# Split products for the last 64 rows of two expert passes, weight buffers dealt anew

## The chip, the cores and the metric

The kernel runs on one core of a Trainium2 chip. The metric is the device time of one execution in microseconds (us). Five engines of the core work side by side, each on its own queue of instructions: TensorE (PE; its weight loads are listed as PEld), VectorE (DVE), ScalarE (ACT), GpSimd (POOL) and SyncE (SP), which only issues DMA transfers. The matrix sums are collected in PSUM, eight banks of 128 x 512 fp32.

## What is computed

The reference takes pooled queries through an attention, sends each of the 1152 resulting rows of 512 values to one of eight experts, and ends in a feed-forward layer. The part around the change is the experts:

```
logits = xc @ w_gate                      # xc: rows with x @ w_skip > 0
e_idx = argmax(logits)
for e in range(8):
    mask = e_idx == e
    h = maximum(xc[mask] @ w1[e], 0.0)    # w1[e]: 512 x 1024
    y[mask] = gate_w[mask] * (h @ w2[e])  # w2[e]: 1024 x 512
out[do_compute] = xc + y
```

All of it is fp32. A matmul with fp32 operands is exact enough; the kernel also uses split products: an operand is the sum of a high and a low half of type fp32r, and three matmuls (high by high, high by low, low by high; the tuple PASS) stand for one.

## The kernel before

The attention ends at about 232 us, the routing and the experts run from there to about 358 us, and the feed-forward layer from there to the end. Rows are sorted into groups of at most 32 rows for each expert (the small groups), and for the experts 0 and 2 into wide passes: 320 rows for expert 0 (two tiles of 128 and a tail of 64), 192 rows for expert 2 (one tile of 128 and a tail of 64). The order of the work on each engine is that of the program text (the schedule is written by hand), and an engine waits for whatever its next instruction needs.

Weights lie in 32 loads of 1 MB, w0 to w31: load n is quarter n % 4 of expert n // 4, the first two quarters W1, the others W2. `place(n)` gives each a buffer, and a load waits until the last reader of the buffer's former content is done. `load_w(first, stop)` issues such loads on SyncE, in that order, so that one that waits holds up those behind it. `whi(e, i)` makes the high half of a quarter on ScalarE, `wlo(e, i)` the low half on VectorE (line 1393), both into spare buffers of the same pool that later loads take over: whi(0, i) in 7 + i, wlo(0, i) in 3 + i, whi(2, i) in 5 + i, wlo(2, i) in 7 + i.

`routing` counts and ranks the rows. It calls `second`, which fetches the rows of the first wide pass on GpSimd, makes wlo(0, 0) and wlo(0, 1), transposes the small rows into xsT[0] and makes the hidden products of the small groups 0 and 1 (`up`, line 645). In `moe`, `turn` transposes such hidden products on TensorE (line 786) and copies them out (line 790); `down`, called by `small2`, multiplies them by W2 (line 807) and adds the two halves on VectorE (line 816); `prep` transposes one tile of a wide pass and makes its high half on ScalarE (line 713) and low half on VectorE (line 714), in the PSUM tag "am", which has two buffers.

`wide` is a loop over nine steps. Step fc makes the hidden products of chunk fc of 128 hidden columns (line 728), runs a hook if one is given for it, and adds the output products of chunk fc - 1 (lines 745 and 750). The hidden products of expert 0 are split products, those of expert 2 plain fp32 ones. The output products of the 128-row tiles are split (line 745: high and low half of the activation are made at lines 733 and 734). Those of the tail are plain fp32 from the raw W2, in two halves of 256 columns that go into the two halves of a PSUM bank's partitions:

```
for half in range(2):
    nc.tensor.matmul(
        acc[J][MID * half : MID * half + MID, :256], g[2],
        wts[e, 2 + fc // 4][:, fc % 4, 256 * half : 256 * half + 256],
```

When a pass ends, its sums are copied out and scattered to the rows of ytok in device memory by GpSimd (line 691), one scatter after another. When the last scatter of expert 2 and that of the small groups 0 to 3 have landed, SyncE loads the first rows of ytok back into yt (line 988), and VectorE adds them to the rows (line 1001), which the feed-forward layer transposes first. Between stand the small groups 4 to 7, which use w16 to w31, and the first loads of the feed-forward weights into a ring (line 1071), whose high halves ScalarE makes and whose low halves VectorE makes (lines 1079 and 1086).

Of the kernel before, what the change touches and what calls it, by code (L numbers as in the profile page):

```python
# [7 lines left out]
F32 = mybir.dt.float32  # L8
F32R = mybir.dt.float32r
AF = mybir.ActivationFunctionType  # L10
ALU = mybir.AluOpType
# [10 lines left out]
P = 128  # L22
# [4 lines left out]
SMALL = 32  # L27
MID = 64
# [10 lines left out]
COL = {r: 2 + i for i, r in enumerate(ROWS)}  # L39
# [441 lines left out]
        nc.tensor.matmul(out, io["ones"], io["blank"], start=True, stop=True)  # L481


def routing(tc, io, lg, rt, tmp, ps, first, second, kept):
    nc = tc.nc
    cst = io["cst"]
    c = lambda n: cst[:, CST[n]]
# [3 lines left out]
    lg = lg[:, :9]  # L491
# [91 lines left out]
    def onehot(cs):  # L583
        n = cs.stop - cs.start
        v = Bm[:, :, cs]
        tt(
            v, c("c128")[:, cs].unsqueeze(1).to_broadcast([P, T, n]),
            hi.unsqueeze(2).to_broadcast([P, T, n]), op=ALU.is_equal,
        )
        tt(v, v, c("tok").unsqueeze(2).to_broadcast([P, T, n]), op=ALU.mult)  # L590
# [9 lines left out]
        column(NEAR, t, ix)  # L600
    nears = tokens(NEAR, ix[:, NEAR])
    keep_warm(nc, io, warm, WARM[5])
    second(idx, ps)
    nc.vector.tensor_copy(cnt[:, :E], count)
    most = sb([P, E + 1], F32, "r_most")
    nc.vector.tensor_copy(most[:, :E], count)
# [3 lines left out]
    nc.vector.tensor_copy(cnt[:, 2 * E :], most[:, E:])  # L610
    stt(cnt[:, E : 2 * E], count, float(-SMALL), thr, op0=ALU.add, op1=ALU.subtract)
    onehot(far)
    ix = ps.tile([P, 512], F32, name="ix", tag="am", bufs=2)
    for t in range(T):
        column(far, t, ix)
# [41 lines left out]
def place(n):  # L657
    if n < 9:
        return 0, n
    if n < 12:  # L660
        return 1, n - 9
    if n < 20:
        return 0, n - 12
    if n < 24:
        return 1, n - 17
    if n < 28:
        return 0, n - 24
    return 1, n - 21


def source(io, e, i):
# [7 lines left out]
def passes(nc, tc, io, r, rows, ytok, wts, ps, wk, nreg, xs, wait=None):  # L679
# [3 lines left out]
    def scatter(src, col, n=P, odd=0):  # L683
        if odd:
            ix = r["odd"][:, col - TAILS.start : col - TAILS.start + 1]
        else:
            ix = r["sidx"][:n, col : col + 1]
        put(src, ix)
# [24 lines left out]
            nc.scalar.copy(xT[:, :, c], tp[:, :, :n])  # L713
            nc.vector.tensor_tensor(lo[:, :, c], tp[:, :, :n], xT[:, :, c].bitcast(F32), op=ALU.subtract)

    def wide(e, xT, w1, w2, outs, hooks):
        J = DEEP[e]
        n = P * J + MID
        two = len(w1) == 2
        acc = [ps.tile([P, 512], F32, name="ly", tag="yl")]  # L720
        acc += [ps.tile([P, 512], F32, name="lt", tag="mt", bufs=2) for _ in range(J)]
        gs = {}

        def hidden(fc):
            a = ps.tile([P, 512], F32, name="la", tag="am", bufs=2)[:, :n]
            prods = [(k, i) for k in range(4) for i in (PASS if two else ((0, 0),))]
            for m, (k, (u, v)) in enumerate(prods):
                nc.tensor.matmul(
                    a, w1[u][k // 2][:, k % 2, P * fc : P * fc + P], xT[v][:, k, :n],
                    start=(m == 0), stop=(m == len(prods) - 1),  # L730
                )
            g = [wk.tile([P, 2 * P], F32R, name=x, tag=x)[:, : P * J] for x in ("wh", "wl")]
            nc.scalar.activation(g[0], a[:, : P * J], AF.Relu)
            nc.vector.scalar_tensor_tensor(
                g[1], a[:, : P * J], 0.0, g[0].bitcast(F32), op0=ALU.max, op1=ALU.subtract
            )
            g.append(wk.tile([P, MID], F32, name="wt", tag="wt"))
            nc.scalar.activation(g[2], a[:, P * J :], AF.Relu)  # L738
            gs[fc] = g

        def outp(fc):
            g = gs.pop(fc)
            for j in range(J):
                for m, (u, v) in enumerate(PASS):
                    nc.tensor.matmul(
                        acc[j], g[u][:, P * j : P * j + P], w2[v][fc // 4][:, fc % 4],
                        start=(fc == 0 and m == 0), stop=(fc == 7 and m == 2),
                    )
            for half in range(2):
                nc.tensor.matmul(  # L750
                    acc[J][MID * half : MID * half + MID, :256], g[2],
                    wts[e, 2 + fc // 4][:, fc % 4, 256 * half : 256 * half + 256],
                    start=(fc == 0), stop=(fc == 7), skip_group_check=True,
                )

        for fc in range(9):
            if fc < 8:
                hidden(fc)
            if fc in hooks:
                hooks[fc]()  # L760
            if fc > 0:
                outp(fc - 1)
        for j in range(J):
            (nc.scalar.copy if j % 2 == 0 else nc.vector.tensor_copy)(outs[j], acc[j])
            scatter(outs[j], COL[e, j])
        for half in range(2):
            (nc.scalar.copy if half else nc.vector.tensor_copy)(
                outs[J][:MID, 256 * half : 256 * half + 256], acc[J][MID * half : MID * half + MID, :256]
            )
        scatter(outs[J][:MID], COL[e, None], MID)  # L770

    def transp(dst, src, alt):
        tp = ps.tile([P, 4, P], F32, name="mt", tag="mt", bufs=2)
# [8 lines left out]
    def turn(M, hs, tag, hT=None):  # L782
        n = M // 16
        tp = ps.tile([P, 4, P], F32, name="ht", tag=tag + "t", bufs=1 if tag == "s" else 2)
        for u in range(n):
            nc.tensor.transpose(tp[:, u], hs[:, P * u : P * u + P], io["ident"])
        if M == SMALL:
            hT = wk.tile([P, n, P], F32, name="hsT", tag="hTs")
        if M == SMALL:
            nc.vector.tensor_copy(hT, tp[:, :n])  # L790
# [100 lines left out]
def moe(tc, io, r, rows, ytok, slot, early, xr, yg, ylast, pick, last, xsT, ps, xm0, hs0, wts, whi, wlo):  # L891
    nc = tc.nc
    with ExitStack() as ctx:
# [42 lines left out]
        def prep0(j):  # L936
            p["prep"](0, j, (xr[:, 1], xr[:, 2], xm0)[j], *xT)

        hT = turn(SMALL, hs0[0], "s")
        prep0(0)  # L940
        small2(0, hT)
        hT = turn(SMALL, hs0[1], "s")
        prep0(1)
        small2(1, hT)
        p["transp"](xsT[1], yg[:, 1], 1)
        gather(yg[:, 1], COL[2, None])
        prep0(2)
        wlo(0, 2)
        wlo(0, 3)
        load_w(12, 14)  # L950
        load_w(16, 20)
        hs = {}

        def next2():
# [5 lines left out]
                p["prep"](2, j, yg[:, j], x2[0])  # L960

        x2 = []
        two = lambda e, i: [[w.w[e, i], w.w[e, i + 1]] for w in (whi, wlo)]
        p["wide"](
            0, xT, two(0, 0), two(0, 2), (xr[:, 1], xr[:, 2], xm0), {2: lambda: r["gates"](r["gate"]), 8: next2}
        )
        load_w(14, 16)
        load_w(20, 24)
        hT = turn(SMALL, hs[2], "s")
        hs[3] = small1(3)  # L970
# [1 line left out]
        for i in (2, 3):  # L972
            wlo(2, i)

        def last3():
            small2(3, turn(SMALL, hs[3], "s"))
            load_w(24, 28)

        def next4():
            hs[4] = small1(4)  # L980

        p["wide"](2, x2, [[wts[2, 0], wts[2, 1]]], two(2, 2), (yg[:, 0], yg[:, 1]), {0: last3, 8: next4})
        load_w(28, 32)
        scatter(ys[0], 0)
        early.open(8)
        nc.sync.dma_start(xr, tiles3(rows, 0))
# [320 lines left out]
def body(tc, io, out):  # L1307
    nc = tc.nc
    with ExitStack() as ctx:
# [59 lines left out]
        with ExitStack() as c2:  # L1369
# [26 lines left out]

            whi.w, wlo.w = {}, {}

            def second(idx, ps):
                fetch(nc, rows, idx, xr[:, 1], COL[0, 0])  # L1400
                fetch(nc, rows, idx, xr[:, 2], COL[0, 1])
                fetch(nc, rows, idx, xm0, COL[0, None])
                wlo(0, 0)
                wlo(0, 1)
                tp = ps.tile([P, 4, P], F32, name="mt", tag="mt", bufs=2)
                for k in range(4):
                    nc.tensor.transpose(tp[:, k], yg[:, 0, P * k : P * k + P], io["ident"])
                nc.scalar.copy(xsT[0], tp)
                for e in range(2):
                    up(nc, ps, hs0[e], SMALL, xsT[0][:, :, SMALL * e : SMALL * e + SMALL], (wts[e, 0], wts[e, 1]), "s")  # L1410

            ps = c2.enter_context(tc.tile_pool(name="m_ps", bufs=1, space=PSUM, reuse_waits="tile"))
            with ExitStack() as c3:
                tmp = c3.enter_context(tc.tile_pool(name="m_rt", bufs=1, reuse_waits="tile"))
                for i in range(4):
                    whi(0, i)
                r = routing(tc, io, lg, rt, tmp, ps, first, second, kept)
# [88 lines left out]
```

## Time and profile before

| what | value |
|---|---|
| time, median of 3 runs | 575.62 us (575.34 to 575.75) |
| the profiled execution | 575.21 us |
| its span, first to last instruction | 573.4 us |
| TensorE busy | 541.2 us, 94% of the span |
| VectorE busy | 389.8 us, 68% |
| ScalarE busy | 372.8 us, 65% |
| DMA | 102.17 MB, mean 178 GB/s |

Busy shares are averages over stages with different limits: in the expert stage TensorE has idle time, in the attention and in the feed-forward layer hardly any. The granted clock of TensorE is given as a share of its full speed of 2.4 GHz; its other level is 1.2 GHz. In a timeline a line of TensorE gives the start, the time to the end, the source line, the tile written and the tiles read, and the form of the array (128\*128, 128\*64, 128\*32). Consecutive matmuls overlap, so the distance from start to start is what one costs, not its own duration. A plain fp32 matmul stands as two records.

### The profile page before, as it was taken

Reading aid. Unit: us, or ns where it says so; the run is one execution under the profiler, and the core shown is the slowest. Engines: PE = TensorE matmul, PEld = TensorE weight load, DVE = VectorE, ACT = ScalarE, POOL = GpSimd, SP = SyncE. Lnnn points to the kernel's source line nnn. Section 1 sums busy time; section 2 is a strip of 40 time slices with the busy share of each in tenths; the row PEclk is TensorE's granted clock in tenths of the full one; section 3 lists DMA queues with packets and bytes.
Section 4 is the critical chain, followed back from the end, with each engine's and each line's share of the span. In section 5 each row is a group of like instructions: output and inputs, shape, how many; then the busy total and the mean of one; then the engine's idle time right before and its main releaser. Section 6 shows DMA issues by size and latency. Waiting matters only on the chain. (4 is left out here: it accounts for less than half of the span.)

```text
span 573.4 us, 11951 instructions
## 1 busy us (share of the span) xinstructions
PE 541.2 (94%) x4788; PEld 405.3 (71%) x4788; DVE 389.8 (68%) x733; ACT 372.8 (65%) x686; POOL 95.7 (17%) x87
## 2 busy tenths in 40 slices
PE   8799999999999999979979969999999999999994
PEld 4566666766676667457746635889899999989882
DVE  3588898888988887863141134799986676666663
ACT  3888888888888885621141222899887667676662
POOL 1223354334533311330001001000000000000000
PEclk9999999999999999999998996999999999999998
DMA  7568868997978771289359594264203100010001
GB/s 259 203 240 280 290 212 285 329 320 250 317 244 302 248 254 58 81 299 390 133 195 404 182 366 150 100 235 135 61 19 102 64 1 1 1 58 0 1 0 60
DMA packets 50113, 102.17 MB, mean 178 GB/s; under 512 B 13995, under 2 KB 15403, under 8 KB 50048
## 3 DMA queue, kind: packets, MB, share of 16 engines
q1 hardware_dynamic: 47760, 95.99, 48.1%
q0 software_dynamic: 1056, 2.97, 1.6%
q10 hardware_dynamic: 1232, 2.36, 1.2%
q8 instruction: 39, 0.64, 0.5%
q14 instruction: 26, 0.21, 0.1%
HBM read 84.70 MB, written 17.04 MB: 177 GB/s over the span
## 5 line engine op out<-in xcount | busy, mean ns | idle before, releaser
L152 DVE TENSOR_SCALAR_CACHE_REDUCE scp<-s 128x1152 f32<-128x1152 f32 x72 | 97.7, 1357 | 34.2 <-PE s L149 20.4
L1187 PE MATMUL ph<-xT,wi 128*128 128x384 f32 x576 | 108.5, 337 | 0.0
L1187 PEld LDWEIGHTS ph<-xT,wi 128*128 128x128 f32 x576 | 102.1, 188 | 4.2
L163 ACT ACTIVATE scp<-scp,mx 128x1152 f32<-128x1152 f32 x72 | 90.5, 1257 | 8.3 <-DVE scp L152 8.1
L149 PE MATMUL s<-ks,qs 64*128 64x288 f32 (+1 forms) x640 | 89.0, 426 | 5.2 <-DVE scp L152 4.9
L1241 PE MATMUL po<-wo,gh 128*128 128x512 f32 x288 | 90.3, 394 | 0.7 <-ACT gh L1226 0.5
L202 ACT COPY eT<-tp 128x1024 f32<-128x1024 f32 x63 | 63.8, 1013 | 27.6 <-PE tp L179 27.0
L220 PE MATMUL ov<-eT,vt 128*64 128x288 f32 x540 | 78.3, 417 | 0.0
L149 PEld LDWEIGHTS s<-ks,qs 64*128 64x128 f32 (+1 forms) x640 | 48.4, 175 | 40.5 <-DVE scp L152 16.6
L1241 PEld LDWEIGHTS po<-wo,gh 128*128 128x128 f32 x288 | 52.9, 188 | 10.2 <-ACT gh L1226 1.4
L1241 PE MATMUL po<-wo,gl 128*128 128x512 f32 x144 | 57.2, 397 | 0.0
L179 PEld LDWEIGHTS tp<-cst,scp 64*128 64x128 f32 x1145 | 47.0, 138 | 13.2 <-issue 3.9
L1211 ACT ACTIVATE u<-u 128x384 f32<-128x384 f32 (+1 forms) x49 | 25.4, 519 | 46.5 <-DVE u L1205 46.0
L1231 DVE TENSOR_TENSOR gl<-s,gh 128x384 fp32r<-128x384 f32 (+1 forms) x49 | 27.0, 550 | 41.7 <-ACT gh L1226 41.5
L351 POOL TENSOR_TENSOR g<-wd 128x512 f32<-128x512 f32 x32 | 34.0, 1062 | 89.0 <-PE s L149 74.8
L179 PE MATMUL tp<-cst,scp 64*128 64x64 f32 x1145 | 48.2, 223 | 0.0
L220 PEld LDWEIGHTS ov<-eT,vt 128*64 128x64 f32 x540 | 33.6, 136 | 19.1
L807 PE MATMUL sy<-w,hsT 128*32 128x256 f32 x256 | 20.3, 472 | 12.4 <-ACT wt L738 4.9
L1241 PEld LDWEIGHTS po<-wo,gl 128*128 128x128 f32 x144 | 27.0, 187 | 6.7 <-DVE gl L1231 1.0
L1205 DVE TENSOR_SCALAR u<-ph 128x384 f32<-128x384 f32 (+1 forms) x49 | 26.7, 546 | 6.4 <-PE ph L1187 6.3
L1213 ACT ACTIVATE r<-s,one 128x384 f32<-128x384 f32 (+1 forms) x49 | 30.0, 612 | 1.6
L1212 ACT ACTIVATE s<-u,one 128x384 f32<-128x384 f32 (+1 forms) x49 | 29.9, 611 | 1.6
(198 smaller groups left out, 752.8 us busy)
## 6 DMA issues: line engine op xcount, KB each, us to landing
w<-w SPq DMA_DIRECT2D x32, 1024.0 KB, 10.3
wd<-wq SPq DMA_DIRECT2D x32, 512.0 KB, 5.1
wdec<-g SPq DMA_DIRECT2D x32, 256.0 KB, 4.3
vt<-vt SPq DMA_DIRECT2D x8, 576.0 KB, 5.9
ks<-kt SPq DMA_DIRECT2D x15, 288.0 KB, 6.9
ring<-wdec SPq DMA_DIRECT2D x16, 256.0 KB, 3.9
wr<-wdec SPq DMA_DIRECT2D x16, 256.0 KB, 2.9
xr<-qt SPq DMA_DIRECT2D x7, 576.0 KB, 5.4
```

What stands on the lines that cost most here:

```text
L149: st["tick"] = nc.tensor.matmul(s[o, half, j, :HQ], w[r], st["k", h, b][r, cs], start=True, stop=True).ins
L152: nc.vector.tensor_scalar(scp.rearrange("p (a c) -> p a c", a=4), s.rearrange("p a j c -> p (a j) c")[:, :, :HQ], -EXP_SCALE, -NEG, op0=AL ...
L163: nc.scalar.activation(scp, scp, AF.Exp, bias=mx, scale=-1.0, accum_out=st["sum", h][:, t : t + 1],)
L179: nc.tensor.matmul(to, e[q, P * i : P * i + P], io["ident"][q, q], start=i < 8 or a != opened, stop=True, is_transpose=True, skip_group_ch ...
L202: nc.scalar.copy(to.rearrange("p k (a c) -> p a k c", a=2), v)
L220: nc.tensor.matmul(acc[D * b : D * b + D, :288], st["v", h][:, b, kc], src[:, kc, b], start=(kc == 0), stop=(kc == KC - 1), skip_group_che ...
L351: side.append(lambda: tt(g, hf, hf, op=ALU.mult))
L1187: nc.tensor.matmul(ph, wi.w[i][:, a, P * k : P * k + P], xTs[c][b][:, k], start=(n == 0), stop=(n == 11),)
L1212: nc.scalar.activation(s[:, c], u[:, c], AF.Square, bias=one)
L1213: nc.scalar.activation(r[:, c], s[:, c], AF.Ln, bias=one)
L1231: nc.vector.tensor_tensor(gl[:, c], a["t"][1][:, c], gh[:, c].bitcast(F32), op=ALU.subtract)
L1241: nc.tensor.matmul(acc[j], g[a][:, P * j : P * j + P], wo[b][:, i], start=(i == 0 and n == 0), stop=(i == 15 and n == 2),)
```

## The change

- The tail of 64 rows takes split products in both wide passes: its activations get a high and a low half together with those of the tiles, and its output products are three matmuls of 512 columns into 64 partitions, in place of two fp32 ones of 256 columns side by side. Nothing in a pass reads the raw W2 any more. The tail's sum is copied out in one piece.
- w28 to w31 take the buffers 1, 2, 0 and 7 of the second pool (before: 7 to 10), that is those of raw W2 and half the raw W1 of expert 2, and one of whi(2, 2).
- The loads are issued in another order: w12 to w15 together ahead of the first pass, w16 to w19 in it, w24 to w29 in the second pass, w30 and w31 behind it.
- `second` is cut in two: wlo(0, 1) and the small groups go into `third`, which stands behind the one-hot work for the far columns. The copy of xsT[0] is in two halves, and the hidden products of group 1 go into a buffer of the tag "am".
- wlo(0, 2) moves ahead of the preparations of the first pass; wlo(0, 3), the turn of small group 1, its W2 products, the transposes of xsT[1] and one gather move into hooks of the first pass. ScalarE copies the first two turned tiles.
- In the second pass the turn of small group 3 stays in hook 0 and its W2 products move to hook 1.

```diff
-    return 1, n - 21
+    return 1, (1, 2, 0, 7)[n - 28]
...
-            g = [wk.tile([P, 2 * P], F32R, name=x, tag=x)[:, : P * J] for x in ("wh", "wl")]
-            nc.scalar.activation(g[0], a[:, : P * J], AF.Relu)
-            nc.vector.scalar_tensor_tensor(
-                g[1], a[:, : P * J], 0.0, g[0].bitcast(F32), op0=ALU.max, op1=ALU.subtract
-            )
-            g.append(wk.tile([P, MID], F32, name="wt", tag="wt"))
-            nc.scalar.activation(g[2], a[:, P * J :], AF.Relu)
+            g = [wk.tile([P, 5 * MID], F32R, name=x, tag=x)[:, :n] for x in ("wh", "wl")]
+            nc.scalar.activation(g[0], a, AF.Relu)
+            nc.vector.scalar_tensor_tensor(g[1], a, 0.0, g[0].bitcast(F32), op0=ALU.max, op1=ALU.subtract)
...
-            for j in range(J):
+            for j in range(J + 1):
+                c = slice(P * j, min(P * j + P, n))
                 for m, (u, v) in enumerate(PASS):
                     nc.tensor.matmul(
-                        acc[j], g[u][:, P * j : P * j + P], w2[v][fc // 4][:, fc % 4],
+                        acc[j][: c.stop - c.start], g[u][:, c], split[v].w[e, 2 + fc // 4][:, fc % 4],
                         start=(fc == 0 and m == 0), stop=(fc == 7 and m == 2),
                     )
-            for half in range(2):
-                nc.tensor.matmul(
-                    acc[J][MID * half : MID * half + MID, :256], g[2],
-                    wts[e, 2 + fc // 4][:, fc % 4, 256 * half : 256 * half + 256],
-                    start=(fc == 0), stop=(fc == 7), skip_group_check=True,
-                )
...
+        wlo(0, 2)
+        hT = turn(SMALL, hs0[0], "s", act=True)
         prep0(0)
         small2(0, hT)
-        hT = turn(SMALL, hs0[1], "s")
         prep0(1)
-        small2(1, hT)
-        p["transp"](xsT[1], yg[:, 1], 1)
-        gather(yg[:, 1], COL[2, None])
         prep0(2)
-        wlo(0, 2)
-        wlo(0, 3)
-        load_w(12, 14)
-        load_w(16, 20)
+        load_w(12, 16)
+
+        def turn1():
+            wlo(0, 3)
+            hs[1] = turn(SMALL, hs0[1], "s", act=True)
+
+        def rest1():
+            small2(1, hs[1])
+            load_w(16, 20)
+
+        def next1():
+            p["transp"](xsT[1], yg[:, 1], 1, "am")
+            gather(yg[:, 1], COL[2, None])
...
+            {0: turn1, 1: rest1, 2: next1, 3: lambda: r["gates"](r["gate"]), 8: next2},
         )
-        load_w(14, 16)
         load_w(20, 24)
...
+        def turn3():
+            hs[3] = turn(SMALL, hs[3], "s")
+
         def last3():
-            small2(3, turn(SMALL, hs[3], "s"))
-            load_w(24, 28)
+            small2(3, hs[3])
+            load_w(24, 30)
...
-        p["wide"](2, x2, [[wts[2, 0], wts[2, 1]]], two(2, 2), (yg[:, 0], yg[:, 1]), {0: last3, 8: next4})
-        load_w(28, 32)
+        p["wide"](2, x2, [[wts[2, 0], wts[2, 1]]], (whi, wlo), (yg[:, 0], yg[:, 1]), {0: turn3, 1: last3, 8: next4})
+        load_w(30, 32)
...
+            def third(ps):
                 wlo(0, 1)
                 tp = ps.tile([P, 4, P], F32, name="mt", tag="mt", bufs=2)
                 for k in range(4):
                     nc.tensor.transpose(tp[:, k], yg[:, 0, P * k : P * k + P], io["ident"])
-                nc.scalar.copy(xsT[0], tp)
+                for k in (0, 2):
+                    nc.scalar.copy(xsT[0][:, k : k + 2], tp[:, k : k + 2])
                 for e in range(2):
-                    up(nc, ps, hs0[e], SMALL, xsT[0][:, :, SMALL * e : SMALL * e + SMALL], (wts[e, 0], wts[e, 1]), "s")
+                    up(
+                        nc, ps, hs0[e], SMALL, xsT[0][:, :, SMALL * e : SMALL * e + SMALL],
+                        (wts[e, 0], wts[e, 1]), "sm"[e],
+                    )
```

## Rows read from the trace of the kernel before

**Rows 1.** Waits of TensorE: who for whom, us in total, times, longest

```profile
PE sy L807 <- ACT hs L650: 4.6, 1, 4.6
...
PE s L149 <- DVE scp L152: 2.0, 2, 1.1
```

**Rows 2.** Table by stretch: length, busy us of each engine, granted clock, DMA share, GB/s

```profile
242.00:256.00 14.00, 10.60 (x157) 6.23 (x157) 9.08 (x26) 4.11 (x10) 5.71 (x8) 1.00 0.72 253
256.00:262.91 6.91, 6.24 (x34) 4.73 (x34) 5.57 (x5) 1.11 (x4) 0.21 (x1) 1.00 1.00 369
...
302.00:305.40 3.40, 3.16 (x32) 1.59 (x32) 0.14 (x1) 0.06 (x1) 1.00 (x1) 0.51 1.04 402
...
342.90:353.10 10.20, 7.96 (x67) 3.35 (x67) 3.04 (x7) 1.53 (x4) 0.98 (x1) 0.50 0.47 174
```

**Rows 3.** Timeline of TensorE, one chunk of the first pass (start us, us)

```profile
262.91 0.42 PE L728 MATMUL la<-xT,wp 128*128 128x320 f32 x1
263.17 0.31 PE L728 MATMUL la<-xTl,wp 128*128 128x320 f32 x1
...
264.79 0.63 PE L745 MATMUL ly<-wp,wh 128*128 128x512 f32 x2
...
265.48 0.63 PE L745 MATMUL lt<-wp,wh 128*128 128x512 f32 x2
...
266.28 0.65 PE L750 MATMUL lt<-w,wt 128*64 128x256 f32 x4
266.86 0.42 PE L728 MATMUL la<-xT,wp 128*128 128x320 f32 x1
```

**Rows 4.** Timeline of TensorE, one chunk of the second pass

```profile
308.39 1.57 PE L728 MATMUL la<-x,w 128*128 128x192 f32 x8
309.66 0.76 PE L745 MATMUL ly<-wp,wh 128*128 128x512 f32 x2
...
310.58 0.65 PE L750 MATMUL lt<-w,wt 128*64 128x256 f32 x4
311.17 0.43 PE L728 MATMUL la<-x,w 128*128 128x192 f32 x1
```

**Rows 5.** Timelines of VectorE and TensorE ahead of the first pass

```profile
239.61 4.49 DVE L1393 TENSOR_TENSOR wp<-w,wp 128x2048 fp32r<-128x2048 f32 x2
...
248.71 0.69 DVE L714 TENSOR_TENSOR xTl<-xt,xT 128x512 fp32r<-128x512 f32 x1
251.07 0.84 DVE L816 TENSOR_TENSOR yg<-sy,yh 32x256 f32<-32x256 f32 x2 [1.66 <-ACT yh L813]
...
256.00 0.42 PE L728 MATMUL la<-xT,wp 128*128 128x320 f32 x1 [0.62 <-ACT xT L713]
```

**Rows 6.** Timeline around TensorE's wait in the second pass

```profile
296.98 0.38 PE L786 MATMUL ht<-cst,hs 128*128 128x128 f32 x2
296.99 4.49 DVE L1393 TENSOR_TENSOR wp<-w,wp 128x2048 fp32r<-128x2048 f32 x2
...
301.72 0.42 DVE L790 COPY hsT<-ht 128x256 f32<-128x256 f32 x1
...
302.24 3.45 PE L807 MATMUL sy<-w,hsT 128*32 128x256 f32 x32 [4.88 <-ACT wt L738]
```

**Rows 7.** Timelines of GpSimd, SyncE and VectorE behind the second pass

```profile
328.79 0.98 POOL L691 DMA_INDIRECT ytok<-yg,sidx  x1 [17.48 <-ACT yg L764]
338.05 0.91 POOL L691 DMA_INDIRECT ytok<-yg,sidx  x1 [8.28 <-ACT yh L813]
343.65 0.98 POOL L691 DMA_INDIRECT ytok<-yg,sidx  x1 [4.68 <-DMA ytok<-yg,sidx]
...
347.48 0.37 SPq L988 DMA_DIRECT2D yt<-ytok  x1
...
352.19 2.08 DVE L1001 SCALAR_TENSOR_TENSOR xr<-yt,gate,xr 128x512 f32<-128x512 f32 x3 [2.85 <-DMA yt<-ytok]
```

**Rows 8.** Groups by line: weight loads of the 128*64 form (busy, mean ns)

```profile
L220 PEld LDWEIGHTS ov<-eT,vt 128*64 128x64 f32 x540 | 33.6, 136 | 19.1
```

More of the change, by code (lines that the diff above doesn't have):

```diff
@@ L481, in keep_warm, with routing @@
         nc.tensor.matmul(out, io["ones"], io["blank"], start=True, stop=True)
-def routing(tc, io, lg, rt, tmp, ps, first, second, kept):
+def routing(tc, io, lg, rt, tmp, ps, first, second, third, kept):
     nc = tc.nc
@@ L602, in routing @@
     keep_warm(nc, io, warm, WARM[5])
-    second(idx, ps)
+    second(idx)
     nc.vector.tensor_copy(cnt[:, :E], count)
@@ L612, in routing @@
     onehot(far)
+    third(ps)
     ix = ps.tile([P, 512], F32, name="ix", tag="am", bufs=2)
@@ L714, in prep, with wide @@
             nc.vector.tensor_tensor(lo[:, :, c], tp[:, :, :n], xT[:, :, c].bitcast(F32), op=ALU.subtract)
-    def wide(e, xT, w1, w2, outs, hooks):
+    def wide(e, xT, w1, split, outs, hooks):
         J = DEEP[e]
@@ L762, in wide, with transp @@
                 outp(fc - 1)
[L763 to L773, printed above, removed]
+        for j in range(J + 1):
+            q = P if j < J else MID
+            (nc.vector.tensor_copy if j % 2 else nc.scalar.copy)(outs[j][:q], acc[j][:q])
+            scatter(outs[j][:q], COL[e, j if j < J else None], q)
+    def transp(dst, src, alt, tag="mt"):
+        tp = ps.tile([P, 4, P], F32, name="mt", tag=tag, bufs=2)
         for k in range(4):
@@ L780, in transp, with turn @@
             nc.vector.tensor_copy(dst, tp)
-    def turn(M, hs, tag, hT=None):
+    def turn(M, hs, tag, hT=None, act=False):
         n = M // 16
@@ L789, in turn @@
         if M == SMALL:
-            nc.vector.tensor_copy(hT, tp[:, :n])
+            (nc.scalar.copy if act else nc.vector.tensor_copy)(hT, tp[:, :n])
         else:
@@ L937, in prep0 @@
             p["prep"](0, j, (xr[:, 1], xr[:, 2], xm0)[j], *xT)
-        hT = turn(SMALL, hs0[0], "s")
+        wlo(0, 2)
+        hT = turn(SMALL, hs0[0], "s", act=True)
         prep0(0)
         small2(0, hT)
-        hT = turn(SMALL, hs0[1], "s")
         prep0(1)
-        small2(1, hT)
-        p["transp"](xsT[1], yg[:, 1], 1)
-        gather(yg[:, 1], COL[2, None])
         prep0(2)
-        wlo(0, 2)
-        wlo(0, 3)
-        load_w(12, 14)
-        load_w(16, 20)
+        load_w(12, 16)
[8 more added lines that the diff above has]
+            gather(yg[:, 1], COL[2, None])
         hs = {}
@@ L962, in moe @@
         x2 = []
-        two = lambda e, i: [[w.w[e, i], w.w[e, i + 1]] for w in (whi, wlo)]
         p["wide"](
-            0, xT, two(0, 0), two(0, 2), (xr[:, 1], xr[:, 2], xm0), {2: lambda: r["gates"](r["gate"]), 8: next2}
+            0, xT, [[w.w[0, i] for i in range(2)] for w in (whi, wlo)], (whi, wlo), (xr[:, 1], xr[:, 2], xm0),
+            {0: turn1, 1: rest1, 2: next1, 3: lambda: r["gates"](r["gate"]), 8: next2},
         )
-        load_w(14, 16)
         load_w(20, 24)
@@ L1397, in body, with second @@
             whi.w, wlo.w = {}, {}
-            def second(idx, ps):
+            def second(idx):
                 fetch(nc, rows, idx, xr[:, 1], COL[0, 0])
@@ L1416, in body @@
                     whi(0, i)
-                r = routing(tc, io, lg, rt, tmp, ps, first, second, kept)
+                r = routing(tc, io, lg, rt, tmp, ps, first, second, third, kept)
             r["gate"] = gate
```

## The prediction

> **What bounds the kernel now.** I read the waits of TensorE first, then a table by stretch, then the timelines of the engines in the expert stage, then the DMA issues. The feed-forward stage that ends the kernel (from 358 us on) is not touched and is bound by TensorE and VectorE, so whatever the expert stage gives back or loses moves the end one for one. So I look only at the expert stage, 242 to 358 us. TensorE has two long waits there, 4.88 us (which the trace puts down to ScalarE, though the real releaser is VectorE, see step 3) and 4.6 us [rows 1, 6]. After each its granted clock is the lower of its two levels, 1.2 GHz: 0.51 of full speed over 302.0 to 305.4 and 0.50 over 342.9 to 353.1 [rows 2]. Its longest other wait in mid-kernel is 1.1 us [rows 1], and the clock stayed up. Ahead of the first wide pass it is busy 10.60 of 14.00 us, and 6.24 of 6.91 us in the first part of that pass [rows 2]: idle together 3.40 + 0.67 = 4.07 us. Inside the passes it has no idle time, and a chunk's length is its matmuls. Last, behind the second pass, three scatters and a load run one after the other, each issued when the one ahead has landed: 328.79, 338.05, 343.65, the load of yt at 347.48, and its reader at 352.19 [rows 7]: 23.40 us. The feed-forward stage cannot begin before that reader. So there are four places to cost.
>
> **Step 1, ahead of the first wide pass: -2.0 us.** The low halves of W2 come apart from the two low halves of W1. One such subtraction is 4.49/2 = 2.25 us on VectorE [rows 5]. Now wlo(0,0) and wlo(0,1) run back to back at 239.61, wlo(0,2) and wlo(0,3) after the preparations. After the change wlo(0,1) stands behind the one-hot work, wlo(0,2) ahead of the first preparation and wlo(0,3) in the pass. VectorE's first low half of x, at 248.71 now [rows 5], then comes near 250: 2.25 us later for wlo(0,2), some 0.4 earlier since ScalarE takes the turned copy, some 0.5 to 0.8 earlier since the hidden products of the two small groups no longer share a PSUM buffer (estimates). Behind it stand 0.69 us, one small group's additions of 0.84 and 0.69 [rows 5], then the pass can have its PSUM buffer: 252.2 against 256.00 now [rows 5]. But 2.9 us of TensorE work (the second small group, the turn of its hidden products, the transposes of xsT[1]) only move from ahead of the pass into it, so the gain is the idle time alone. Of 4.07 us I leave 2.1: TensorE still waits for VectorE's low halves between the transposes and the first chunk. -2.0, with ends at -0.8 (the chain on VectorE a subtraction longer) and -3.4. The hidden cover: wlo(0,3) lies beside the second chunk and the small group; it is needed only from chunk 4 on. SyncE's queue: w14 and w15 now go out ahead of w16, and w15 waits for wlo(0,3), with w16 to w19 queued behind it until some 257; they are read after 285 at the earliest, so this costs nothing.
>
> **Step 2, the tail of 64 rows in both passes: +2.6 us.** Now it is two fp32 halves of 256 columns side by side in the 128*64 form; after it is three matmuls of 512 columns with a 64-column weight. In the first pass a chunk starts at 262.91 and the next at 266.86: 3.95 us. Three f32r matmuls of 512 columns take 0.69 (264.79 to 265.48), the next three up to the tail 0.80, the tail 0.58 (266.28 to 266.86), and the first matmul after the tail 0.26 where eleven others take 1.62/11 = 0.147 [rows 3]. So going into the 128*64 form costs 0.11 and coming out another 0.11 at least. In the second pass the tail takes 0.59 as well (310.58 to 311.17), out of a chunk of 2.78 [rows 4], with fp32 on either side of it, so it is the form and not the type that costs. The new tail also has 64 columns, and I take it that it keeps the form and both switches. Its three matmuls cost 2 x 0.23 and a last one of about 0.28, together 0.74: +0.16 a chunk, 16 chunks, +2.6 us. The low end is 3 x 0.23 = 0.69 without any switch: 0.11 + 0.58 + 0.11 = 0.80 now, so -0.11 a chunk, -1.8 us; the upper end is the slow rival below. I take +2.6 since the nearest rows are those of the same form.
> The Trainium skill speaks against this edit: TensorEngine Tiling (Array Packing), "Theoretical Speedup", says that a matmul with 64 or fewer columns of weight can run up to twice as fast by sharing the array with another, which is just what the old tail does and the new one does not; FP8 and Floating Point Precision counts four passes for true fp32. By those two pages the old tail is an estimated 256 x 4 columns at 2.4 GHz, 0.43 us, the new one 3 x 512, 0.64: +0.21 a chunk, +3.4 us in all. The rows, 0.58 for the old tail, make the loss smaller.
>
> **Step 3, the wait in the second pass: -1.3 us.** TensorE is out of work at 297.36 and resumes at 302.24. It needs the turned copy at 301.72, which stands on VectorE behind wlo(2,2) and wlo(2,3), 296.99 for 4.49 us [rows 6]. Nothing of that order is changed: from the end of the second small group to the copy it is the same chain. But the small group now comes one hook later, so chunk 1's hidden products, which follow it today, fill the wait: 308.39 to 309.66, 1.27 us [rows 4]. The wait becomes 3.6 us. Whether the clock falls in it is not shown: it fell in 4.88 and 4.6 us, and held in 1.1 [rows 1, 6]. 3.6 is nearer to the former (their middle is 2.85), so I take a fall, which costs what it costs today: nothing is won. If it holds, about half of 3.16 busy us [rows 2] are won, -1.55.
> ScalarE in place of VectorE for the first two turned copies, and single evictions of the tail in place of halves: neither engine is late there; nothing. Also nothing: xsT copied in halves (0.2 us, in step 1's idle time).
>
> **Step 4, behind the second pass: -4.0 us.** Today w28 waits for a buffer of the second pass, w29 to w31 go out at its end, and the four ring loads queue behind them. All that runs while the first scatter is in flight, and it lasts to its successor 9.26 us, the second 5.60, the third, with the queues nearly empty, 3.83 [rows 7]. After the change w14, w15 and w20 to w29 have landed long before, since their buffers come free earlier (no raw W2 is read inside the passes); only w30, w31, the ring and xr go out, some 4 us before the pass ends, when its last hidden products have freed w[2,0] and w[2,1]. So the first scatter shares the DMA engines for about 5 us and then not: I take 7.0 for it, 4.0 for the second (64 rows), 3.83 for the third and 4.71 for yt as now: 19.5 against 23.4, so -3.9, and 0.1 for a first copy that no longer ends behind the tail. Ends: all three scatters at 3.83 (-7.2), or the first still at 9.26 (-1.6). TensorE's own work is no longer than this: the 4.6 us wait was for hidden products queued on ScalarE behind a ring load [rows 1], and falls away with the ring landed early; with it goes the lower clock (7.96 busy us in 342.9 to 353.1, worth 4.0 [rows 2]). So its work ends 8.6 us sooner in its stretch, less about 1 us for two low halves of the ring on VectorE, and then it waits some 3 us for yt. Whether the clock falls in that is undecided: 3 us is near the middle of 1.1 and 4.6, and the ends of the chain make it 0 to 5. I take no fall and give the fall as a rival. The chain of scatters is what is late next.
>
> **The sum.** -2.0 + 2.6 - 1.3 - 4.0 = -4.7 us. The profiled execution took 575.21 us (span 573.4): it would be 570.5. The median of the runs is 575.62, 0.41 above, so the forecast is 570.9.
>
> **The rivals.**
> - The clock holds in the shorter wait of step 3: -1.55 more, 569.3. For it: the wait is a quarter shorter; against: it fell twice in waits of this order. Chance 0.20.
> - The new tail keeps no separate form: -1.8 in place of +2.6, 566.5; half of it, 568.7. For it: nothing runs beside it in the array. Against: every narrow matmul of this trace has its own form. Chance 0.10.
> - The wait for yt brings the clock down again, as the 4.6 us wait did: the transposes and products ahead of the feed-forward stage then start slow, and half of some 4 us of work at 0.50 is lost, as half of 3.16 was [rows 2]: +2.0, 572.9. For it and against it: the wait of about 3 us lies between those that are known. Chance 0.15.
> - The change does not do what it says behind the second pass: the scatters stay as long, because their time is not the loads' doing, and step 4 gives only 0.5: 574.4 to 575, within the measurement. Against: 9.26 with loads in flight and 3.83 without. Chance 0.10.
> - Slower: in the 128*64 form each tail matmul waits for its own weights. Price: a weight load of that form is 0.136 us [rows 8], 48 tail matmuls, +6.5: 577.4. It turns the result from 0.124 us a matmul on (5.9 us over 48). Against: the weights of the other output matmuls are twice as wide and hide wholly behind the 0.23 us of the matmul ahead [rows 3]. Chance 0.08.
> - The forecast: 0.37.
>
> **The range.** The terms' ends and the cases give 566.8 to 574.2. It leaves out the slow case, most of the case without effect, and the far end of a tail without switches. Faster or slower by over 0.2% (1.15 us, about what a measurement of this kernel can tell) follow from the cases: faster 0.37 + 0.20 + 0.10 + 0.15 = 0.82, same 0.10, slower 0.08.
>
> **What would show it.** Step 1: the first wide matmul near 252 and three TensorE pieces inside the pass. Step 2: the tail as three 128*64 matmuls, a chunk of 4.1 us in the first pass and 2.94 in the second. Step 3: an idle time of 3.6 us ahead of the small group's matmuls in the second pass, at lower clock after it. Step 4: the reader of yt 19 to 20 us behind the first scatter, no ring load in ScalarE's way, and TensorE waiting for yt rather than for hidden products. The prediction is wrong if the tail's form costs nothing or twice as much, if VectorE's chain ahead of the first pass is longer than I laid out, or if the scatters do not shorten.

## The result and the profile after

The changed kernel takes 567.04 us (median of 4, 566.1 to 571.7) against 575.68 of the kernel before on the same chip: a ratio of 0.9858 (95% interval 0.9809 to 0.9907), 1.4% faster, which is 8.2 us by the ratio and 8.6 by the medians. In a second comparison the ratio was 0.9819 (0.9783 to 0.9856). The forecast was 570.9 in a range of 566.8 to 574.2. Sign and range held, but the median lies only 0.2 us above the low end of the range, and one of the four terms had the wrong sign.

The profiled execution is the longest of this kernel's executions, 571.70 us with a span of 569.9; its routing began 0.6 us later than in the profile before (wlo(0,0) at 240.21 against 239.61), which is to be taken off each point in time of this profile.

The chunks, to be held against [rows 3, 4]: TensorE's timeline in the first and the second pass.

```profile
266.49 0.31 PE L729 MATMUL la<-xT,wp 128*128 128x320 f32 x1
266.64 0.31 PE L729 MATMUL la<-xTl,wp 128*128 128x320 f32 x1
...
268.96 0.62 PE L743 MATMUL lt<-wp,wh 128*128 128x512 f32 x2
...
269.65 0.63 PE L743 MATMUL lt<-wp,wh 128*64 128x512 f32 x2
270.11 0.40 PE L743 MATMUL lt<-wp,wl 128*64 128x512 f32 x1
270.35 0.31 PE L729 MATMUL la<-xT,wp 128*128 128x320 f32 x1
...
309.18 1.47 PE L729 MATMUL la<-x,w 128*128 128x192 f32 x8
310.35 0.75 PE L743 MATMUL ly<-wp,wh 128*128 128x512 f32 x2
...
311.17 0.63 PE L743 MATMUL lt<-wp,wh 128*64 128x512 f32 x2
311.63 0.39 PE L743 MATMUL lt<-wp,wl 128*64 128x512 f32 x1
311.86 1.46 PE L729 MATMUL la<-x,w 128*128 128x192 f32 x8
```

A chunk is 3.86 us long (3.95 before) and 2.68 (2.78). The tail stands in the 128\*64 form and takes 0.70 (269.65 to 270.35); the step into it is no longer than any other (268.96 to 269.65 for three matmuls), and the first matmul behind it takes 0.15, as all others (270.35, then 270.49). In the second pass the hidden products behind a tail take 1.17 (309.18 to 310.35) where they took 1.27. There is no switch.

Ahead of the first pass, against [rows 5]: VectorE, then TensorE.

```profile
244.84 2.29 DVE L1390 TENSOR_TENSOR wp<-w,wp 128x2048 fp32r<-128x2048 f32 x1
...
248.08 2.28 DVE L1390 TENSOR_TENSOR wp<-w,wp 128x2048 fp32r<-128x2048 f32 x1
250.28 0.68 DVE L715 TENSOR_TENSOR xTl<-xt,xT 128x512 fp32r<-128x512 f32 x1
```

```profile
251.01 0.46 PE L709 MATMUL xt<-cst,xm 64*128 64x64 f32 x4 [0.77 <-DVE xTl L715]
252.57 0.38 PE L729 MATMUL la<-xT,wp 128*128 128x320 f32 x1 [1.10 <-DVE xTl L715]
```

The pass starts at 252.57 (252.0 without the shift) against 256.00. The shorter wait in the second pass, against [rows 6], with VectorE's copy that ends it:

```profile
300.99 0.41 DVE L778 COPY hsT<-ht 128x256 f32<-128x256 f32 x1
...
301.51 3.32 PE L795 MATMUL sy<-w,hsT 128*32 128x256 f32 x32 [3.65 <-issue]
```

Behind the second pass, against [rows 7]: GpSimd, SyncE, VectorE, and TensorE's wait.

```profile
326.43 0.98 POOL L692 DMA_INDIRECT ytok<-yg,sidx  x1 [20.64 <-ACT yg L757]
333.19 0.91 POOL L692 DMA_INDIRECT ytok<-yg,sidx  x1 [5.77 <-DVE hsT L778]
336.73 1.48 POOL L692 DMA_INDIRECT ytok<-yg,sidx  x1 [2.63 <-DMA ytok<-yg,sidx]
...
341.74 0.37 SPq L985 DMA_DIRECT2D yt<-ytok  x1
...
346.40 2.08 DVE L998 SCALAR_TENSOR_TENSOR xr<-yt,gate,xr 128x512 f32<-128x512 f32 x3 [4.76 <-DMA yt<-ytok]
...
347.21 5.49 PE L1127 MATMUL ft<-cst,xr 128*128 128x128 f32 x24 [3.58 <-DVE xr L998]
```

From the first scatter to the reader of yt it is 19.97 us (23.40 before), and TensorE, done earlier, waits 3.58 us for it. The last view is the table by stretch, against [rows 2] (length, busy us of PE, PEld, DVE, ACT and POOL, granted clock, DMA share, GB/s):

```profile
242.60:256.60 14.00, 11.77 (x138) 8.48 (x139) 10.96 (x24) 4.43 (x11) 7.79 (x7) 0.91 0.52 174
...
254.10:257.50 3.40, 3.40 (x16) 3.36 (x15) 1.92 (x2) 0.80 (x2) 0.00 (x0) 0.50 1.03 401
301.90:305.30 3.40, 3.40 (x32) 1.85 (x22) 0.00 (x0) 0.36 (x1) 0.91 (x2) 0.50 0.21 82
346.30:353.10 6.80, 5.89 (x25) 5.62 (x26) 4.12 (x7) 0.00 (x0) 0.98 (x1) 0.50 0.50 155
```

The clock is at its lower level, 1.2 GHz, three times: behind the waits of 0.77 and 1.10 us, of 3.65 and of 3.58. By these rows the three falls cost an estimated 5.6 us: half of 3.40 busy us, 1.4 for the small group (3.32 where it takes 1.93 at full clock, as a run below shows) and 2.55 for the transposes (5.49 where they take 2.94). That is about as much as this profile is longer than the other executions.

### The profile page after: what moved, and what is told of

It is laid out like the page before. It is cut to its first block, busy times and chain, and to the rows that moved or that the text cites. A ratio compares the mean times of both kernels' runs of the same rounds, so it can differ in the third digit from the quotient of the medians.

```text
span 569.9 us, 11889 instructions
## 1 busy us (share of the span) xinstructions
PE 540.2 (95%) x4770; PEld 412.9 (72%) x4772; DVE 389.9 (68%) x730; ACT 370.6 (65%) x672; POOL 99.0 (17%) x87
## 5 line engine op out<-in xcount | busy, mean ns | idle before, releaser
L734 ACT ACTIVATE wh<-la 128x320 fp32r<-128x320 f32 (+1 forms) x16 | 6.2, 386 | 41.8 <-PE la L729 41.8
L735 DVE SCALAR_TENSOR_TENSOR wl<-la,wh 128x320 fp32r<-128x320 f32 (+1 forms) x16 | 6.8, 424 | 36.4 <-ACT wh L734 36.3
```

## The experiments

**The same kernel again.** 

> The changed kernel once more. Its first profiled execution took 571.7 us at a mean granted clock of 0.983 of full speed, its other executions 566.1 to 567.2 at 0.990 to 0.994. If the falls of the clock in the three shortened waits (in the first pass, in the second pass, ahead of the feed-forward stage) come and go from one execution to the next, this profile has fewer than three of them, and a time near 567. If they belong to the kernel, it has three again and the time of a profiled execution is near 571.

 Its profile took 569.75 us, with two falls (299.9 and 344.3) and none in the first pass. Its table by stretch around the waits there, and what follows them:

```profile
249.70:252.70 3.00, 1.13 (x11) 0.78 (x9) 2.96 (x6) 1.32 (x3) 1.68 (x4) 1.00 0.25 67
253.50:257.00 3.50, 3.50 (x31) 3.21 (x33) 1.74 (x2) 0.92 (x3) 0.00 (x0) 1.00 1.00 397
```

The waits ahead of the first pass are the same, the clock behind them is not. Its other executions, with their mean clock, were 564.79 (0.993), 565.57 (0.993) and 568.41 (0.988); those of the first comparison 571.70 (0.983), 567.19 (0.994), 566.88 (0.990) and 566.10 (0.991). The fall in the first pass comes and goes, then. The two others are in both profiles; the mean clocks say that some executions have less of the lower clock than these profiles, but not which fall they lack. The time goes with the mean clock only roughly (567.19 at 0.994, 566.10 at 0.991).

**The tail alone**, the new `wide` in the old order of work.

```diff
-            for j in range(J):
+            for j in range(J + 1):
+                c = slice(P * j, min(P * j + P, n))
...
```

> The kernel before with the split tail of 64 rows alone; loads, buffers and the order of all other work as before. By step 2 of the prediction (the 128*64 form costs a switch each way): chunks of 4.1 and 2.94 us, +2.6, about 578.2. By the rows of the kernel after (chunks of 3.86 and 2.69 us, no switch): -0.09 us a chunk, 16 chunks, -1.5, about 574.2.

 Measured: 575.58, ratio 0.9984 (0.9967 to 1.0001). That is neither number. Chunks are as short as in the kernel after, so TensorE has an estimated 1.5 us less to do, but the chain behind the second pass is as long as before: first scatter at 328.71, reader of yt at 352.44, 23.7 us. In the profile the clock stayed low longer in the second pass (299.4 to 306.2, 6.8 us in place of 3.4): the small group takes 3.64 in place of 3.45 and the hidden products behind it 1.42 in place of 1.26, which is 0.35 us of the gain. Where the rest goes is open, and the clock does not settle it: the two executions with the highest mean clock (0.988 and 0.989) took 575.91 and 574.98, the four at 0.981 between 575.32 and 575.87.

**fp32 tail, not side by side**, in the kernel before:

```diff
-            for half in range(2):
-                nc.tensor.matmul(
-                    acc[J][MID * half : MID * half + MID, :256], g[2],
...
+            nc.tensor.matmul(
+                acc[J][:MID], g[2], wts[e, 2 + fc // 4][:, fc % 4], start=(fc == 0), stop=(fc == 7),
+            )
```

> The kernel before with the plain fp32 tail as one matmul of 512 columns into 64 partitions, in place of two of 256 columns side by side in the two halves of the array. It keeps fp32 and the 128*64 form, and gives up only the halves side by side. If the switch of 0.11 us each way belongs to the form 128*64 or to fp32, it is there still. If it belongs to running two halves side by side, the first f32r matmul behind the tail costs 0.15 and the step into the tail 0.23, as in the kernel after. The tail itself should take 2 x 0.43 us in place of 0.52, so the time is worse, about 0.1 to 0.35 us a chunk.

 One execution: 581.77 us, against a median of 575.47. The tail takes 1.00 us (267.80 to 268.80) in place of 0.58 (not 0.52, as the expectation has it), so a chunk loses 0.42, more than was expected. TensorE's timeline:

```profile
267.47 0.40 PE L745 MATMUL lt<-wp,wl 128*128 128x512 f32 x1
267.80 1.07 PE L749 MATMUL lt<-w,wt 128*64 128x512 f32 x2
268.80 0.42 PE L728 MATMUL la<-xT,wp 128*128 128x320 f32 x1
269.05 0.31 PE L728 MATMUL la<-xTl,wp 128*128 128x320 f32 x1
```

The step in takes 0.33 and the first matmul behind the tail 0.25, as with two halves. So it is not the halves. It is not the form either, since fp32r in the same form (kernel after) has neither step. And it is not the change of type: in the second pass of the kernel after, the narrow tail is fp32r and the hidden products behind it fp32 in the full form, and the step between them is 0.23 (311.63 to 311.86), while in the kernel before fp32 followed on fp32 there and the 0.1 us was lost. What costs 0.1 us each way is fp32 in the narrow form.

The weight loads show where that time lies (PEld): the kernel before, then the kernel after.

```profile
266.27 0.20 PEld L750 LDWEIGHTS lt<-w,wt 128*64 128x64 f32 x4 [0.37 <-ACT wt L738]
266.86 0.19 PEld L728 LDWEIGHTS la<-xT,wp 128*128 128x128 f32 x1 [0.39 <-issue]
...
269.42 0.36 PEld L743 LDWEIGHTS lt<-wp,wh 128*64 128x64 f32 x2
270.11 0.19 PEld L729 LDWEIGHTS la<-xT,wp 128*128 128x128 f32 x1
```

In the kernel after, the weights of the tail and of the matmul behind it begin to load one matmul ahead, 0.23 us before the matmul that uses them (269.65 and 270.35). In the kernel before both loads begin only with their own matmul (266.28 and 266.86), so here they are not hidden. The activation that the trace names is not what held the tail up, since behind the last chunk, where none is near, the step is 0.33 too (290.70 to 291.03). Why narrow fp32 weights are not loaded ahead is open.

**Tail and loads**: also the new buffers and the new order of the loads.

```diff
-    return 1, n - 21
+    return 1, (1, 2, 0, 7)[n - 28]
...
-        load_w(12, 14)
-        load_w(16, 20)
+        load_w(12, 20)
...
-        load_w(14, 16)
...
-            load_w(24, 28)
+            load_w(24, 30)
...
-        load_w(28, 32)
+        load_w(30, 32)
```

> The kernel before with the split tail and the new dealing and order of the weight loads (w12 to w19 ahead of the first pass, w24 to w29 in the second, w30 and w31 behind it), all other work in the old order. If the loads set how long the scatters take (step 4), the reader of yt comes 19 to 20 us behind the first scatter in place of 23.4, and the time is 1.5 + 4 below the kernel before, about 570. If they do not, it is that of the tail alone, about 574.

 Measured: 569.81, ratio 0.9893 (0.9862 to 0.9924), 5.8 below the tail alone by the medians (5.2 by the ratios). That the scatters do not depend on the loads is refuted. The chain in this kernel, GpSimd, SyncE and VectorE:

```profile
329.49 0.98 POOL L691 DMA_INDIRECT ytok<-yg,sidx  x1 [21.45 <-ACT yg L756]
336.58 0.91 POOL L691 DMA_INDIRECT ytok<-yg,sidx  x1 [6.11 <-issue]
339.79 1.05 POOL L691 DMA_INDIRECT ytok<-yg,sidx  x1 [2.30 <-DMA ytok<-yg,sidx]
...
342.48 0.37 SPq L972 DMA_DIRECT2D yt<-ytok  x1
...
347.19 2.08 DVE L985 SCALAR_TENSOR_TENSOR xr<-yt,gate,xr 128x512 f32<-128x512 f32 x3 [2.31 <-DMA yt<-ytok]
```

From the first scatter to the reader of yt it is 17.7 us in place of 23.4: 7.09, 3.21 and 2.69 for the scatters, 4.71 for yt. TensorE's wait for a ring load is 1.2 us (5.6 with the tail alone), and the clock stays up there.

**The order ahead of the first pass alone**, tail and loads as before. 

> The kernel before with only the order ahead of and inside the first pass changed (wlo(0,1) behind the one-hot work, wlo(0,2) ahead of the preparations, wlo(0,3), small group 1 and the transposes of xsT[1] in hooks); old tail, old buffers, w14 and w15 behind the pass as before. By step 1: the pass begins near 252, the time is 2.0 lower, 573.6. Rival: the clock falls in the first pass as it did in the profile of the kernel after (0.83 over 252 to 262) and takes 1.6 back: about 575.2.

 Measured: 573.95, ratio 0.9972 (0.9952 to 0.9993), -1.6 us by the ratio. The pass began near 253 (the routing 1.1 us later than in the profile before), and in this profile too the clock was low over 253.0 to 256.4. The executions lie in two groups, six from 573.4 to 574.0 and four from 576.4 to 577.7, and the profiled one is in the upper. The gain stands, and the fall in some executions is part of what the median shows.

**Small group 3 back in hook 0**, in the kernel after:

```diff
-        def turn3():
-            hs[3] = turn(SMALL, hs[3], "s")
...
-            small2(3, hs[3])
+            small2(3, turn(SMALL, hs[3], "s"))
```

> The kernel after with the W2 products of small group 3 put back into hook 0 of the second pass. By step 3 the wait ahead of them grows from 3.65 us to 4.9, since the hidden products of chunk 1 no longer fill it: +1.3, about 568.3 where the kernel after takes 567.0. If the clock is what counts there and it falls with the longer wait in every execution, up to 1.5 more, 569.8. Rival: the wait only moves, since outputs wait for the same low half wlo(2,2): no difference.

 Measured: 569.42, ratio 0.9869 (0.9836 to 0.9902), 2.4 above the first median of the kernel after. The wait is the one expected, and the clock was low for 6.8 us at its end and behind it (301.0 to 307.8):

```profile
301.94 3.64 PE L795 MATMUL sy<-w,hsT 128*32 128x256 f32 x32 [4.95 <-issue]
```

The interval contains one ratio of the kernel after (0.9858) and overlaps the interval of the other, and this profile differs elsewhere too: from the first scatter to the reader of yt it is 17.97 us, and the clock stays up ahead of the feed-forward stage. So only the wait, not its price, is shown.

**Matmuls of no use in that wait**, in the kernel after:

```diff
+            warm = ps.tile([P, 512], F32, name="warm", tag="ys")
+            keep_warm(nc, io, warm, 13)
             small2(3, hs[3])
```

> The kernel after with 13 bf16 matmuls of 512 columns of no use (about 0.23 us each, 3.0 us) put into the wait of 3.65 us ahead of small group 3. If the fall of the clock there costs what step 3 says, the profile shows 2.4 GHz over 299 to 306, the small group's matmuls take 1.9 us and not 3.3, and executions that had this fall gain 1.5 us: about 565.5 to 566.5. Rival: the matmuls draw on what the following work needs, or the fall comes anyway: 567 or more.

 Measured: 566.25, ratio 0.9815 (0.9780 to 0.9851). The clock was 1.00 over 296 to 303, and the small group took 1.93 us:

```profile
299.85 1.93 PE L795 MATMUL sy<-w,hsT 128*32 128x256 f32 x32 [0.84 <-PE warm L481]
```

So a fall here costs 1.4 us (3.32 less 1.93). In the median little of it is seen, and the interval overlaps both of the kernel after. Why is open: all three profiles in which this wait of 3.65 us is left empty (both of the kernel after and that of the next run) have the fall, and of the other executions only the mean clock is known.

**A scatter less in the chain**, in the kernel after: that of the small groups 0 to 3 goes out in the pass.

```diff
             load_w(24, 30)
+            scatter(ys[0], 0)
...
-        scatter(ys[0], 0)
         early.open(8)
```

> The kernel after with the scatter of the small groups 0 to 3 moved from behind the second pass into its hook 1, right behind the last addition into its rows. By step 4 the chain of scatters is what is late behind the second pass, and this takes one of its three off it: the reader of yt comes 15 to 16 us behind the first scatter in place of 20, TensorE no longer waits for it (3.5 us in the profile of the kernel after) and the clock does not fall there. About -3.5 against executions without a fall, more against those with one: 563 to 564. Rival: the load of yt or the ring is what is late, and nothing is won: 567.

 Measured: 564.54, ratio 0.9796 (0.9772 to 0.9821), 2.5 below the first median of the kernel after; the interval overlaps that of its second ratio (0.9819), so the size is uncertain; that the wait is gone, the trace shows. The reader of yt comes 15.8 us behind the first scatter (324.54 in this profile) and now waits for nothing in VectorE's queue, and TensorE goes from the last small group to the transposes without a wait:

```profile
340.36 2.08 DVE L998 SCALAR_TENSOR_TENSOR xr<-yt,gate,xr 128x512 f32<-128x512 f32 x3
...
340.39 1.93 PE L795 MATMUL sy<-w,hsT 128*32 128x256 f32 x32 [1.49 <-DVE hsT L778]
342.25 2.94 PE L1127 MATMUL ft<-cst,xr 128*128 128x128 f32 x24
```

**The same in the kernel before.** 

> The same move in the kernel before. There TensorE's own work behind the second pass (with its wait of 4.6 us for a ring load and its half clock) ends at 353.0, as late as the reader of yt can use it. If chain and work are level, taking a scatter off the chain brings the reader of yt forward by about 3.8 us and the end by 0.6 at most: 575.5. If the chain alone were late there: -3.5, 572.5.

 Measured: 576.09, ratio 0.9993 (0.9976 to 1.0009): nothing. The reader waits for nothing here either, but TensorE is not done earlier:

```profile
345.27 3.64 PE L807 MATMUL sy<-w,hsT 128*32 128x256 f32 x32 [4.69 <-ACT hs L650]
...
350.77 3.64 PE L807 MATMUL sy<-w,hsT 128*32 128x256 f32 x32 [1.24 <-DVE hsT L790]
354.35 2.94 PE L1130 MATMUL ft<-cst,xr 128*128 128x128 f32 x24
```

The chain and TensorE's own work, with its wait for the ring and its half clock, were level in the kernel before, where TensorE began the transposes at 353.00, 0.81 us behind the reader of yt [rows 7]. The loads shorten both, the scatter only one.

**All together.** Early scatter and matmuls in the wait: 

> The kernel after with both the early scatter of small groups 0 to 3 and the 13 matmuls in the wait of the second pass. If the two act in different places (clock at 300 us, chain behind the pass), they add: early scatter 564.5, and about 0.7 to 1.5 off it for executions whose clock fell at 300: 563. If the rest of the spread comes from elsewhere (the clock in the first pass, the attention), they do not add: 564.5.

 Measured: 562.24, ratio 0.9768 (0.9746 to 0.9790), mean clocks 0.993 to 0.996, no fall between 100 us and the last products in its profile. That is nearer to the sum (563) than to 564.5, but its interval overlaps that of the early scatter alone. Then the ring's split behind small group 7:

```diff
-            if e == 6:
-                early.split(2)
...
         p["put"](ys[1], last)
+        early.split(2)
```

> The same, and the split of the first two ring tiles no longer ahead of small group 7 but behind its turn, and the second two behind the last additions. In the kernel with the early scatter TensorE waits 1.6 and 1.5 us around there for copies that stand behind this split on ScalarE and VectorE. If TensorE's own work is what is late there now, the first wait goes and 1 to 1.5 us are won: about 562. Rival: VectorE's chain (turned copy, low halves, additions) is as late, and it stays at 563.

 Measured: 561.75, ratio 0.9751 (0.9727 to 0.9774). The wait for ScalarE is gone, the one for VectorE is not, and the two ratios cannot be told apart. Last, the preparations ahead of wlo(0,2):

```diff
-        wlo(0, 2)
         hT = turn(SMALL, hs0[0], "s", act=True)
         prep0(0)
-        small2(0, hT)
         prep0(1)
+        small2(0, hT)
         prep0(2)
+        wlo(0, 2)
```

> The kernel with early scatter, matmuls in the wait and the late ring, and ahead of the first pass wlo(0,2) behind the last preparation and the W2 products of small group 0 behind the second. In the kernel after TensorE waits 0.77 and 1.10 us there for low halves that stand behind wlo(0,2) on VectorE, and in some executions the clock falls behind these waits (0.50 of full speed over 254.1 to 257.5 in one profile, 1.00 in another). If wlo(0,2) on VectorE sets the start of the pass (step 1), these waits shrink to about 1 us together, the pass starts 1 us earlier and the clock holds: 561.75 - 1.0 and less spread, about 560.7. Rival: the transposes of the third tile and its copies are as late, and it stays at 561.7.

 Measured: 561.15, ratio 0.9727 (0.9703 to 0.9752), executions from 560.1 to 561.95. The two waits ahead of the pass became 0.4, 0.5 and 0.2, the first now for a fetch:

```profile
251.26 0.43 PE L709 MATMUL xt<-cst,xm 64*128 64x64 f32 x4 [0.38 <-DMA xm<-rows,idx]
252.15 0.42 PE L729 MATMUL la<-xT,wp 128*128 128x320 f32 x1 [0.46 <-ACT xT L714]
```

Against the step before it the gain is within the intervals; against the kernel before this is the fastest, 2.7%.

## Why the prediction was right, and where it was not

- **Step 1, -2.0.** Right: -1.6 alone (about 0.4 to 2.8 by its interval), with the start of the pass at 252.0 where 252.2 was forecast. Missed: that the clock can fall there. A wait of 1.1 us was held to be safe, but behind the two waits of about 0.8 and 1.1 us the clock fell in four of the eight profiles that have them and held in the other four.
- **Step 2, +2.6.** Wrong in sign: the term is -1.5 (16 chunks by 0.09 to 0.10). The step that failed is "it is the form and not the type that costs", and by the prediction's own sign ("wrong if the tail's form costs nothing") it failed outright: fp32r in that form costs nothing going in or out, and the 0.1 us each way goes with fp32 in it, whose weights were not loaded ahead. The prediction read "fp32 on either side" of the tail in the second pass; fp32 stands only behind it, and ahead of it stand split products of type fp32r (line 745). The tail itself was fp32 in both passes, so [rows 3, 4] could not tell form from type. The low end, "without any switch" (-1.8), was nearly the case.
  The estimate of +3.4 from the Trainium skill (TensorEngine Tiling (Array Packing), "Theoretical Speedup", and FP8 and Floating Point Precision, "TensorE Precision Notes") has the wrong sign too, and the measurement decides. The bare tail did grow, from 0.58 to 0.70, but the steps into it and out of it went.
- **Step 3, -1.3.** The wait came out at 3.65 (3.6 forecast), and taken back at 4.95. The fall of the clock that was forecast is in every profile that leaves the wait empty, and is worth 1.4.
- **Step 4, -4.0.** Right in kind. On top of the tail alone the loads bring more than was forecast, 5.8. In that kernel the chain is 17.7 and not 19.5, since the second and third scatters take 3.21 and 2.69 where I took 4.0 and 3.83. In the kernel after it is 19.97, near the forecast, with 5.01 for the third scatter (336.73 to 341.74). Why that one is so long is open: GpSimd issues it beside VectorE's low half of a ring tile (336.05 to 337.34, 1.48 us for the issue), but so it does in the kernel with tail and loads (339.29 to 340.58), where the scatter takes 2.69.
- **The rivals.** The tail without a switch was one (0.10), and its 566.5 is nearest to the 567.04 measured, though not for its reason: the new tail does keep the narrow form. The fall ahead of the feed-forward stage was another (0.15): it is there in both profiles of the kernel after (5.49 us for transposes that take 2.94). That the clock holds in step 3 is in neither. Slower weights in the new tail, and scatters that do not depend on loads, are refuted.
- **The sum.** Alone or by difference: order ahead of the pass -1.6, tail -0.6 (not told apart from nothing), loads -5.8, hook -1.3 by its wait, together -9.3, where the two comparisons gave -8.2 and -10.4 (0.9819 of 576). So the parts add within what was measured. The forecast was 3.9 us too high. Step 2 is most of that: 4.1 us by the chunks, 3.2 by the time of the tail alone (-0.6 where +2.6 was forecast). That the time still lies in the range is in part luck: the range left out the far end of a tail without switches, which is what happened, and the second comparison would put the time at 566.99 by its median, but near 565.3, outside, by its ratio.

## What to carry to other kernels

When a cost shows at the border between two kinds of instruction, list every way in which they differ, and look for a row in which only one of them changes, before the cost is put down to one. When a chain of transfers and an engine's own work end at the same time, shortening one alone can give nothing (576.09 here, with the chain shortened), and a change that shortens both can give much (569.81). Short waits can cost more than their length when a fall of the clock follows: compare executions by their mean granted clock before a difference of 1% is explained.

## What the hardware showed that was not expected

- fp32 matmuls with 64 columns of weight cost about 0.1 us more going in and coming out (0.33 and 0.25 against 0.23 and 0.15), whether one or two lie side by side, and the weight loads at both borders begin only with their own matmul; fp32r ones of the same form cost nothing more, and their weights load one matmul ahead.
- GpSimd takes 2.74 us to issue the fetch of xm and 2.93 for that of yg where they run beside a subtraction of 2.29 and 2.28 us on VectorE, and 1.27 and 0.95 for the same two where they do not (GpSimd's timeline of the kernel before, then of the kernel after):

```profile
245.22 1.27 POOL L633 DMA_INDIRECT xm<-rows,idx  x1 [0.30 <-issue]
246.80 0.95 POOL L633 DMA_INDIRECT yg<-rows,idx  x1 [0.30 <-issue]
...
243.62 1.27 POOL L634 DMA_INDIRECT xr<-rows,idx  x1 [0.30 <-issue]
245.20 2.74 POOL L634 DMA_INDIRECT xm<-rows,idx  x1 [0.30 <-issue]
248.24 2.93 POOL L634 DMA_INDIRECT yg<-rows,idx  x1 [0.30 <-issue]
```

Each of the two ends 0.81 us behind the subtraction (244.84 and 248.08, shown above). The Trainium skill, SBUF — State Buffer, "SBUF: two separate sides", has it that VectorE and GpSimd share a pair of ports that one holds for a whole instruction, and that a VectorE instruction with two inputs in SBUF takes it only against a GpSimd instruction that reads SBUF. These rows agree: the subtraction has both inputs in SBUF, and the fetch reads its indices there. The change moved two subtractions onto two fetches. That put off the weight loads behind them by about 2.8 us (SyncE issues the first at 251.28 in place of 247.86); TensorE waited for one of the fetches themselves, that of xm, only where the preparations were brought forward (0.38 us).
